# Finer steps in the opening of an attention and feed-forward kernel: a cell's maximum, high part and output product a slot behind its first product

## The chip, the cores and the metric

The kernel runs on one core of one Trainium2 chip. The metric is the device time of one execution, in microseconds, as the median over runs. TensorE is called PE here, VectorE DVE, ScalarE ACT, GpSimd POOL, and SP is the engine whose queue issues nearly all DMAs.

## The reference

Sliding-window attention (8 batches, 8 heads, 576 positions, head size 64, window 64) is followed by a feed-forward layer with a leaky rectifier over all 4608 tokens:

```python
scores = scale * np.matmul(q, k.transpose(0, 1, 3, 2))
mask = (rel >= 0) & (rel < 64)                  # rel = query position - key position
scores = np.where(mask, scores, -1e9)
attn = softmax(scores)                          # with 1e-9 added to the sum
x = (attn @ v) -> (4608, 512)
h = x @ w_in                                    # 512 x 2048
g = np.maximum(h, 0.0) + alpha * np.minimum(h, 0.0)
out = (g @ w_out).astype(np.float32)            # 2048 x 512
```

`w_in` and `w_out` arrive as 64-bit floats, so the kernel reads each weight as two 32-bit halves and rebuilds it. Products are made in a 32-bit format of reduced precision, so every factor is split into a high and a low part and a product is three matmuls: low by high, high by low, high by high.

## The kernel before

The 4608 tokens are 36 tiles of 128. Tiles are grouped into blocks of two (blocks 0, 1 and 2) and three (the ten others). The feed-forward work of a block is 16 cells, one for each 128 of the 2048 hidden columns.

A cell is made of these pieces: `m_hidden` (12 matmuls, tile `h`, line 304), `m_slopes` (ACT multiplies by the scaled slopes, line 313, then DVE takes the maximum, line 314, tile `g`), `m_split` (ACT copies the high part `gh`, line 323, POOL subtracts it for `gl`, line 324) and `m_out` (for each tile of the block three matmuls into `o`, line 338; `gl` is read first).

Weights come in 32 chunks of 512 KB, even ones of `w_in`, odd ones of `w_out`; chunks 2f and 2f+1 belong to cell f. A chunk is fetched into `raw` (three buffers, SP's queue), then turned into 32-bit parts: `mask_exp` (DVE masks the exponent bits into `two`, line 123, ACT rescales them, line 125), `mask_man` (DVE `man`, line 130, ACT, line 133), `join` (DVE `exp`, line 140, and `val`, line 142; two buffers each), `product` (POOL, line 148), `high_part` (ACT, line 159, `win_h` or `wout_h`) and `low_part` (POOL, line 163, `win_l` or `wout_l`).

Attention of a tile: `a_score` (32 matmuls of half the array, in two halves of 16), `a_soft` for each of eight groups (DVE adds the mask and takes the least, line 223; ACT exponentiates and sums, line 226), `a_norm` (DVE adds 1e-9 and inverts, lines 232 and 233; POOL scales `w`, line 234), for the first six tiles `a_transpose_pe` (four PE transposes and an ACT copy for each half), and `a_value` (32 matmuls, ACT copies `xh`, line 262, DVE subtracts for `xl`, line 263).

The opening covers attention of tiles 0 to 5, all 32 chunks, and blocks 0 and 1. In it every engine, and SP's queue, gets its instructions in the order in which the program calls these functions (`tc.manual_schedule()`); an instruction waits for the one ahead of it on its engine even where its own data are there. After a written-out start for tiles 0 and 1, a loop over slots j = 3, 4, ... handles in each slot one chunk's masks, the join and product of the chunk before, high and low part of the one before that, zero to two cells, and one of five attention steps (`STEPS`) of tiles 2 to 5. The first step of a tile also issues the eight loads of the next tile on SP's queue, behind that slot's `fetch`. Block 1's cells begin ten slots after block 0's; until it has caught up there are two cells in a slot. Behind the opening only PE's order is written out, and the blocks 2 to 12 run with the weights resident.

Three PSUM pools matter: `ps_h` (two banks, shared by `h` and `two`), `ps_a` (three banks, shared by `man`, attention's tiles and the output tile `o_3`) and `ps_o` (three banks).

Of the kernel before, what the change touches and what calls it, by code (L numbers as in the profile page):

```python
# [8 lines left out]
F32 = mybir.dt.float32  # L9
# [16 lines left out]
def banded_attention_then_prelu_ffn(  # L26
# [93 lines left out]
    def mask_exp(c):  # L120
        d = cv[c]
        d["two"] = two = ps_h.tile([P, E], I32, tag="ph", name=f"two_{c}")
        nc.vector.tensor_scalar(out=two, in0=d["high"], scalar1=0x7FF00000, scalar2=None,  # L123
                                op0=ALU.bitwise_and)
        nc.scalar.activation(two, two, AF.Relu, scale=8.0, bias=ebias)  # L125

    def mask_man(c):
        d = cv[c]
        d["man"] = man = ps_a.tile([P, E], I32, tag="psa", name=f"man_{c}")
# [3 lines left out]
        nc.scalar.activation(man.bitcast(F32), man, AF.Copy,  # L133
                             scale=s20_sb[:, c // 2:c // 2 + 1] if c % 2 else 2.0**-20)

    def join(c):
        d = cv[c]
        d["val"] = val = io.tile([P, E], F32, tag="val", name=f"val_{c}", bufs=2)
        d["exp"] = exp = io.tile([P, E], I32, tag="exp", name=f"exp_{c}", bufs=2)
        nc.vector.scalar_tensor_tensor(out=exp, in0=d["high"], scalar=-2**31, in1=d["two"],  # L140
                                       op0=ALU.bitwise_and, op1=ALU.bitwise_or)
        nc.vector.scalar_tensor_tensor(out=val, in0=d["low"],
                                       scalar=s52_sb[:, c // 2:c // 2 + 1] if c % 2 else 2.0**-52,
                                       in1=d["man"].bitcast(F32), op0=ALU.mult, op1=ALU.add)
# [72 lines left out]
    def a_soft(t, g):  # L217
# [3 lines left out]
        w, nm = d["w"][:, g, :], d["nm"][:, g:g + 1]  # L221

        nc.vector.tensor_tensor_reduce(  # L223
            out=w, in0=d["s"][u % len(d["s"])][:, e], in1=mask, op0=ALU.add, op1=ALU.min,
            scale=-SCALE, scalar=3.0e38, accum_out=nm)
        nc.scalar.activation(w, w, AF.Exp, scale=-1.0, bias=nm, accum_out=d["sm"][:, g:g + 1])  # L226

    def a_norm(t, halves=(0, 1)):
# [3 lines left out]
        nc.vector.tensor_scalar_add(rc, d["sm"][:, g], 1e-9)  # L232
        nc.vector.reciprocal(rc, rc)  # L233
        nc.gpsimd.tensor_tensor(out=w, in0=w, in1=rc.unsqueeze(2).broadcast_to(list(w.shape)),  # L234
                                op=ALU.mult)

# [7 lines left out]
    def a_transpose_pe(t, u):  # L244
        tp = a_bank(t, f"t_{t}_{u}")
        for e in range(NP):
            nc.tensor.transpose(tp[:, e], st[t]["w"][:, u * NP + e, :], ident)  # L247
        nc.scalar.copy(pts[t % 2][:, u * NP:(u + 1) * NP, :], tp)

    def a_value(t):  # L250
# [4 lines left out]
        for e in range(NP):  # L255
            for u in range(2):
                for h in range(2):
                    r = slice(h * D, (h + 1) * D)
                    nc.tensor.matmul(av[r, e, u * W:(u + 1) * W], v[:, e, u, r],  # L259
                                     pt[:, u * NP + e, h * W:(h + 1) * W], start=True, stop=True)  # L260
        xs = slice((place[n] + i) * P, (place[n] + i + 1) * P)
        nc.scalar.copy(xh[:, :, xs], av)
        nc.vector.tensor_tensor(out=xl[:, :, xs], in0=av, in1=xh[:, :, xs].bitcast(F32), op=ALU.subtract)  # L263
        st.pop(t)

    def eighth(s):
# [17 lines left out]
        elif k == 7:  # L284
# [3 lines left out]
            if last:  # L288
                a_value(t - 1)
            if t + 1 < NT:  # L290
                v_load(t + 1)
# [17 lines left out]
    def m_slopes(n, f):  # L309
# [3 lines left out]
        nc.scalar.activation(g, ph[:, :nt], AF.Copy, scale=sa_sb[:, f:f + 1])  # L313
        nc.vector.scalar_tensor_tensor(out=g, in0=ph[:, :nt], scalar=s_sb[:, f:f + 1], in1=g,  # L314
# [40 lines left out]
    def cell(n, f):  # L355
        m_hidden(n, f)
        m_slopes(n, f)
        m_split(n, f)
# [10 lines left out]
    def load(t):  # L369
# [4 lines left out]
    STEPS = [  # L374
        lambda t: (load(t + 1), a_score(t, (0,)), soft(t, 0)),
        lambda t: (a_score(t, (1,)), soft(t, 1), a_norm(t, (0,))),
        lambda t: (a_norm(t, (1,)), a_transpose_pe(t, 0)),
        lambda t: (a_transpose_pe(t, 1),),
        lambda t: (a_value(t),),
    ]  # L380
    LEAD = 3

    def opening():
# [43 lines left out]
        a_value(1)  # L427

        done, wait = [0, 0], []
        first = [0, 5 * sizes[1]]  # L430
        j = LEAD
        while done != [NF, NF] or wait:

            ready = [n for n in range(2) if j - LEAD >= first[n]]
            at = min(NF, (j - LEAD) // 2 + 1)
            behind = sum(at - done[n] for n in ready)
            cells = []
            for _ in range(min(behind, 2 if behind > 2 else 1)):
# [36 lines left out]
            j += 1  # L475

# [61 lines left out]
```

## Time and profile before

| | |
|---|---|
| median of 3 runs | 976.8 us (976.49 to 978.27) |
| profiled execution | 977.33 us, span 975.5 us, mean granted clock 0.99 |
| busy over the span | PE 922.1 us, DVE 463.1, ACT 423.6, POOL 350.8 |
| opening, up to its last output product | 184.0 us, PE busy 138.1 us in it |
| behind it, to the end of the span | 791.5 us, PE busy 783.9 us in it |

Times in the profile are microseconds from the start of the span. A row of the table of stages gives a stretch, its length, the busy time of each engine with its number of instructions, the granted PE clock as a share of full speed, the mean busy share of the 16 DMA engines and GB/s. A row of the chain of waits gives a start, a duration and the piece of work that the end is traced back to; "issue" is time in which nothing that the profile shows was waited for. A row of a timeline gives start, duration, engine, line, operation, written and read tile, and in brackets the idle time before it and who ended it.

### The profile page before, as it was taken

The page shows a single profiled execution, that of the slowest core. Times are in us where ns is not written, and L with a number is a line of the kernel's source. Part 1 is how long each engine was busy: PE and PEld are TensorE (multiplying, and loading weights), DVE is VectorE, ACT ScalarE, POOL GpSimd, SP SyncE. Part 2 cuts the span into 40 slices and gives each one's busy share as a digit, 9 for nine tenths or more (in the row PEclk, how much of TensorE's full clock was granted, in tenths as well). Part 3 has the DMA queues.
Part 4 walks back from the last instruction along what each step waited for, and adds up shares of the span by engine and source line. Part 5 has one row for each costly group of instructions (what it writes and reads, how often), then busy time and mean ns, then how long its engine had stood idle before and what let it go on. Part 6 is the DMA issues. An engine that isn't in the chain of part 4 may idle for free.

```text
span 975.5 us, 17299 instructions
## 1 busy us (share of the span) xinstructions
PE 922.1 (95%) x6576; PEld 815.7 (84%) x6576; DVE 463.1 (47%) x1394; ACT 423.6 (43%) x1174; POOL 350.8 (36%) x327
## 2 busy tenths in 40 slices
PE   4667988999999999999999999999999999999998
PEld 3456867778898898889889889889988988989997
DVE  3675678576444444444444444444444444441111
ACT  4565676635433433433433443443443344332322
POOL 3575779533233233233233223223223222322221
PEclk9989999999999999999999999999999999999999
DMA  9866284324333233233233233233233232000000
GB/s 212 166 166 150 85 207 141 104 60 93 76 65 62 64 68 64 65 64 65 64 65 65 63 65 65 61 64 69 59 70 64 61 67 53 34 22 1 33 1 33
DMA packets 96418, 74.53 MB, mean 76 GB/s; under 512 B 44624, under 2 KB 89680, under 8 KB 96336
## 3 DMA queue, kind: packets, MB, share of 16 engines
q1 hardware_dynamic: 94272, 73.42, 32.2%
q8 instruction: 52, 0.85, 0.4%
q10 hardware_dynamic: 2064, 0.01, 0.1%
q14 instruction: 30, 0.25, 0.1%
HBM read 63.97 MB, written 9.44 MB: 75 GB/s over the span
## 4 chain that ended last, share of the span: by engine, by line
PE 84%; ACT 6%; DVE 4%; POOL 2%; issue 2%; DMA 1%; SPq 1%; POOLq 0%; ACTq 0%; DVEq 0%
PE h L304 38%; PE o L338 38%; PE s L209 4%; PE av L259 4%; ACT w L226 2%; DVE pt L242 1%; DVE two L123 1%; ACT two L125 1%; ACT g L313 1%; POOL w L234 1%; PE t L247 1%; ACT man L133 1%; ACT gh L323 1%; DMA v<-vN 1%; DVE g L314 1%
## 5 line engine op out<-in xcount | busy, mean ns | idle before, releaser
L324 POOL TENSOR_TENSOR gl<-g,gh 128x384 fp32r<-128x384 f32 (+1 forms) x208 | 196.9, 947 | 428.5 <-ACT gh L323 333.3
L314 DVE SCALAR_TENSOR_TENSOR g<-h,s_sb,g 128x384 f32<-128x384 f32 (+1 forms) x208 | 122.1, 587 | 332.7 <-ACT g L313 329.8
L338 PE MATMUL o<-wout_h,gl 128*128 128x512 f32 x576 | 228.3, 396 | 14.7 <-POOL gl L324 14.7
L338 PE MATMUL o<-wout_l,gh 128*128 128x512 f32 x576 | 229.1, 398 | 0.0
L338 PE MATMUL o<-wout_h,gh 128*128 128x512 f32 x576 | 226.6, 393 | 0.0
L313 ACT ACTIVATE g<-h,sa_sb 128x384 f32<-128x384 f32 (+1 forms) x208 | 115.4, 555 | 251.4 <-PE h L304 251.4
L304 PE MATMUL h<-xh,win_l 128*128 128x384 f32 (+1 forms) x832 | 177.6, 336 | 13.8 <-DVE g L314 6.4
L242 DVE STREAM_TRANSPOSE pt<-w 32x256 f32<-32x256 f32 x360 | 157.0, 436 | 64.2 <-POOL w L234 59.1
L323 ACT CAST gh<-g 128x384 fp32r<-128x384 f32 (+1 forms) x208 | 101.4, 487 | 185.4 <-DVE g L314 185.3
L304 PEld LDWEIGHTS h<-xh,win_l 128*128 128x128 f32 x832 | 141.3, 190 | 36.7 <-DVE g L314 11.9
L304 PE MATMUL h<-xl,win_h 128*128 128x384 f32 (+1 forms) x832 | 169.7, 325 | 0.0
L304 PE MATMUL h<-xh,win_h 128*128 128x384 f32 (+1 forms) x832 | 168.8, 324 | 0.0
L304 PEld LDWEIGHTS h<-xl,win_h 128*128 128x128 f32 x832 | 143.4, 189 | 0.2 <-DVE xl L263 0.2
L304 PEld LDWEIGHTS h<-xh,win_h 128*128 128x128 f32 x832 | 140.6, 190 | 0.0
L338 PEld LDWEIGHTS o<-wout_h,gl 128*128 128x128 f32 x576 | 109.2, 190 | 32.6 <-POOL gl L324 16.0
L226 ACT ACTIVATE w<-w,nm 128x128 f32<-128x128 f32 x288 | 112.3, 392 | 55.7 <-DVE nm L223 55.6
L338 PEld LDWEIGHTS o<-wout_h,gh 128*128 128x128 f32 x576 | 109.5, 190 | 24.4
L234 POOL TENSOR_TENSOR w<-w,rc 128x1024 f32<-128x1024 f32 (+1 forms) x40 | 69.0, 1726 | 160.8 <-DVE rc L233 151.8
L338 PEld LDWEIGHTS o<-wout_l,gh 128*128 128x128 f32 x576 | 109.4, 190 | 14.4
L223 DVE CUSTOM_DVE_ANT_0 w<-s,masks 128x128 f32<-128x128 f32 x288 | 64.1, 286 | 64.4 <-PE s L209 64.3
L209 PEld LDWEIGHTS s<-k,q 64*64 64x64 f32 x1152 | 38.0, 138 | 26.4 <-PE o L338 11.1
L209 PE MATMUL s<-k,q 64*64 64x128 f32 x1152 | 49.5, 285 | 11.1 <-DMA q<-qT 9.0
(43 smaller groups left out, 509.6 us busy)
## 6 DMA issues: line engine op xcount, KB each, us to landing
k<-kT SPq DMA_DIRECT2D x72, 256.0 KB, 4.6
v<-vN SPq DMA_DIRECT2D x72, 256.0 KB, 4.7
q<-qT SPq DMA_DIRECT2D x144, 64.0 KB, 4.3
out<-os SPq DMA_DIRECT2D x36, 256.0 KB, 2.1
raw<-w_in SPq DMA_DIRECT2D x16, 512.0 KB, 4.4
raw<-w_out SPq DMA_DIRECT2D x16, 512.0 KB, 3.6
alpha_sb<-alpha ACTq DMA_DIRECT2D x1, 8.0 KB, 4.6
```

The lines of the kernel that those rows point to most:

```text
L209: nc.tensor.matmul(d["s"][u - halves[0]][out_, e], q[r, e, h, :], k[r, e, :, h, :], start=True, stop=True)
L223: nc.vector.tensor_tensor_reduce(out=w, in0=d["s"][u % len(d["s"])][:, e], in1=mask, op0=ALU.add, op1=ALU.min, scale=-SCALE, scalar=3.0e38 ...
L226: nc.scalar.activation(w, w, AF.Exp, scale=-1.0, bias=nm, accum_out=d["sm"][:, g:g + 1])
L234: nc.gpsimd.tensor_tensor(out=w, in0=w, in1=rc.unsqueeze(2).broadcast_to(list(w.shape)), op=ALU.mult)
L242: nc.vector.transpose(pt[ks, :, r], w[r, :, ks])
L259: nc.tensor.matmul(av[r, e, u * W:(u + 1) * W], v[:, e, u, r], pt[:, u * NP + e, h * W:(h + 1) * W], start=True, stop=True)
L304: nc.tensor.matmul(ph[:, :nt], wt[:, c, fs], xt[:, c, xs], start=(k == 0), stop=(k == 3 * NP - 1))
L313: nc.scalar.activation(g, ph[:, :nt], AF.Copy, scale=sa_sb[:, f:f + 1])
L314: nc.vector.scalar_tensor_tensor(out=g, in0=ph[:, :nt], scalar=s_sb[:, f:f + 1], in1=g, op0=ALU.mult, op1=ALU.max)
L323: nc.scalar.copy(gh, g)
L324: nc.gpsimd.tensor_tensor(out=gl, in0=g, in1=gh.bitcast(F32), op=ALU.subtract)
L338: nc.tensor.matmul(po[t], gt[:, ts], wt[:, f, :], start=(f == 0 and k == 0), stop=(f == NF - 1 and k == 2))
```

## The change

The opening's order is written anew from smaller pieces; what is computed is the same. `a_soft` becomes `a_least` and `a_exp`, `a_norm` becomes `a_inverse` and `a_scale`, `a_transpose_pe` becomes `a_turn` and `a_turned`, `a_value` gives up its two evictions to `a_xh` and `a_xl`, `m_slopes` gives up the maximum to `m_larger`, and the two masks of a chunk are one function, `masks_of`. In the new loop

- a cell's first product is issued at the end of a slot, its slopes at the start of the next, its maximum and split in the middle of that one, and its output product in a later slot (a second cell of a slot is done within it, at the end);
- a chunk's masks and join stand in one slot, its product, high and low part in the next;
- an attention step's PE part comes first in its slot, DVE's least in the middle, ACT's part near the end.

The start for tiles 0 and 1 is reordered too, and the small operations on `alpha` go ahead of the first softmax. A second call of `high_part(1)` and `low_part(1)`, which the loop before made in its first slot, is gone. The core of the diff, new functions first:

```diff
+    def step(t, k):
+        G = range(NP)
+        u = k % 2
+        if k < 2:
+            return dict(pe=lambda: a_score(t, (u,)),
+                        inverse=(lambda: a_inverse(t, (0,))) if k else None,
+                        scale=(lambda: a_scale(t, (0,))) if k else None,
+                        least=lambda: [a_least(t, u * NP + e) for e in G],
+                        act=lambda: [a_exp(t, u * NP + e) for e in G],
+                        dma=(lambda: load(t + 1)) if not k else None)
+        if k < 4:
+            return dict(pe=lambda: a_turn(t, u), act=lambda: a_turned(t, u),
+                        inverse=(lambda: a_inverse(t, (1,))) if k == 2 else None,
+                        scale=(lambda: a_scale(t, (1,))) if k == 2 else None)
+        return dict(pe=lambda: a_value(t), act=lambda: a_xh(t), last=lambda: a_xl(t))
...
         fetch(1)
         v_load(1)
         fetch(2)
+        nc.vector.tensor_scalar(out=s_sb, in0=alpha_sb, scalar1=1.0, scalar2=-2.0, op0=ALU.is_gt, op1=ALU.mult)
+        nc.vector.tensor_scalar_add(s_sb, s_sb, 1.0)
+        nc.vector.tensor_tensor(out=sa_sb, in0=s_sb, in1=alpha_sb, op=ALU.mult)
+        nc.vector.tensor_scalar_mul(s20_sb, s_sb, 2.0**-20)
+        nc.vector.tensor_scalar_mul(s52_sb, s_sb, 2.0**-52)
         a_score(0)
         soft(0, 0)
         soft(0, 1)
-        mask_exp(0)
-        mask_man(0)
-        a_norm(0)
-        nc.vector.tensor_scalar(out=s_sb, in0=alpha_sb, scalar1=1.0, scalar2=-2.0, op0=ALU.is_gt, op1=ALU.mult)
-        nc.vector.tensor_scalar_add(s_sb, s_sb, 1.0)
-        nc.vector.tensor_scalar_mul(s20_sb, s_sb, 2.0**-20)
-        nc.vector.tensor_scalar_mul(s52_sb, s_sb, 2.0**-52)
-        nc.vector.tensor_tensor(out=sa_sb, in0=s_sb, in1=alpha_sb, op=ALU.mult)
+        a_norm(0, (0,))
+        masks_of(0)
+        a_norm(0, (1,))
+        a_turn(0, 0)
+        a_turned(0, 0)
+        a_score(1)
+        soft(1, 0)
         join(0)
+        product(0)
         fetch(3)
-        product(0)
-        a_score(1)
-        a_transpose_pe(0, 0)
-        a_transpose_pe(0, 1)
+        load(2)
+        a_turn(0, 1)
+        a_turned(0, 1)
+        soft(1, 1)
+        a_norm(1, (0,))
+        a_norm(1, (1,))
+        a_value(0)
         high_part(0)
-        soft(1, 0)
-        soft(1, 1)
-        a_value(0)
         low_part(0)
-        mask_exp(1)
-        mask_man(1)
-        a_norm(1)
-        load(2)
+        masks_of(1)
+        a_xh(0)
+        a_xl(0)
+        a_turn(1, 0)
+        a_turned(1, 0)
+        a_turn(1, 1)
+        a_turned(1, 1)
         join(1)
+        product(1)
         fetch(4)
-        product(1)
-        mask_exp(2)
-        mask_man(2)
-        a_transpose_pe(1, 0)
-        a_transpose_pe(1, 1)
+        a_value(1)
+        a_xh(1)
+        a_xl(1)
         high_part(1)
         low_part(1)
-        a_value(1)
-
-        done, wait = [0, 0], []
-        first = [0, 5 * sizes[1]]
+        masks_of(2)
+        join(2)
+        fetch(5)
+
+        done = [0, 0]
+        first = [0, LEAD + 5 * sizes[1]]
+        wait = []
+
+        def pick(j):
+            ready = [n for n in range(2) if j >= first[n] and 2 * done[n] + 2 <= j and done[n] < NF]
+            if not ready:
+                return None
+            n = min(ready, key=lambda n: done[n])
+            done[n] += 1
+            return n, done[n] - 1
+
+        def behind(j):
+            return sum(min(NF, j // 2) - done[n] for n in range(2) if j >= first[n])
+
+        def output(j):
+            if wait and 2 * wait[0][1] + 3 <= j:
+                m_out(*wait.pop(0))
+
+        todo = pick(LEAD - 1)
+        m_hidden(*todo)
         j = LEAD
-        while done != [NF, NF] or wait:
-
-            ready = [n for n in range(2) if j - LEAD >= first[n]]
-            at = min(NF, (j - LEAD) // 2 + 1)
-            behind = sum(at - done[n] for n in ready)
-            cells = []
-            for _ in range(min(behind, 2 if behind > 2 else 1)):
-                n = min(ready, key=lambda n: done[n])
-                cells.append((n, done[n]))
-                done[n] += 1
-            if cells:
-                m_hidden(*cells[0])
-            if 0 <= j - 2 < 2 * NF:
-                high_part(j - 2)
-            if j - 1 < 2 * NF:
-                join(j - 1)
-            fetch(j + 2)
-            if j - 2 < 2 * NF:
-                low_part(j - 2)
-            if cells:
-                m_slopes(*cells[0])
+        while todo or wait or j <= 2 * NF:
+            t, k = divmod(j - LEAD, 5)
+            att = step(t + 2, k) if t + 2 < EARLY else {}
+            part = lambda name: (att.get(name) or (lambda: None))()
+            part("pe")
+            if todo:
+                m_slopes(*todo)
+            if j < 2 * NF:
+                masks_of(j)
             if j - 1 < 2 * NF:
                 product(j - 1)
+            part("inverse")
+            part("scale")
+            output(j)
+            if todo:
+                m_larger(*todo)
+                m_split(*todo)
+                wait.append(todo)
+            part("least")
+            if j - 1 < 2 * NF:
+                high_part(j - 1)
+                low_part(j - 1)
             if j < 2 * NF:
-                mask_exp(j)
-            if cells:
-                m_split(*cells[0])
-            if j < 2 * NF:
-                mask_man(j)
-            if wait and 2 * wait[0][1] + 1 + LEAD <= j:
-                m_out(*wait.pop(0))
-            for c in cells[1:]:
-                m_hidden(*c)
-                m_slopes(*c)
-                m_split(*c)
-                if wait and 2 * wait[0][1] + 1 + LEAD <= j:
-                    m_out(*wait.pop(0))
-            wait += cells
+                join(j)
+
+            if behind(j - 1) > 1:
+                more = pick(j - 1)
+                m_hidden(*more)
+                output(j)
+                m_slopes(*more)
+                m_larger(*more)
+                m_split(*more)
+                wait.append(more)
+            todo = pick(j)
+            if todo:
+                m_hidden(*todo)
             while len(wait) > 2:
                 m_out(*wait.pop(0))
-            t, k = divmod(j - LEAD, 5)
-            if t + 2 < EARLY:
-                STEPS[k](t + 2)
+            part("act")
+            part("last")
+            fetch(j + 3)
+            part("dma")
             j += 1
+        assert done == [NF, NF] and not wait
 
     with tc.manual_schedule():
         opening()
```

More of the change, by code (lines that the diff above doesn't have):

```diff
@@ L118, in fetch, with masks_of @@
         cv[c] = dict(low=raw[:, :, 0].bitcast(U32), high=raw[:, :, 1])
-    def mask_exp(c):
+    def masks_of(c):
         d = cv[c]
         d["two"] = two = ps_h.tile([P, E], I32, tag="ph", name=f"two_{c}")
+        d["man"] = man = ps_a.tile([P, E], I32, tag="psa", name=f"man_{c}")
         nc.vector.tensor_scalar(out=two, in0=d["high"], scalar1=0x7FF00000, scalar2=None,
@@ L125, in mask_exp @@
         nc.scalar.activation(two, two, AF.Relu, scale=8.0, bias=ebias)
-    def mask_man(c):
-        d = cv[c]
-        d["man"] = man = ps_a.tile([P, E], I32, tag="psa", name=f"man_{c}")
         nc.vector.tensor_scalar(out=man, in0=d["high"], scalar1=0xFFFFF, scalar2=0x100000,
@@ L137, in join @@
         d = cv[c]
-        d["val"] = val = io.tile([P, E], F32, tag="val", name=f"val_{c}", bufs=2)
         d["exp"] = exp = io.tile([P, E], I32, tag="exp", name=f"exp_{c}", bufs=2)
@@ L141, in join @@
                                        op0=ALU.bitwise_and, op1=ALU.bitwise_or)
+        d["val"] = val = io.tile([P, E], F32, tag="val", name=f"val_{c}", bufs=2)
         nc.vector.scalar_tensor_tensor(out=val, in0=d["low"],
@@ L215, in a_score, with a_least @@
             d["rc"] = wk.tile([P, NH], F32, tag="rc", name=f"rc_{t}")
-    def a_soft(t, g):
+    def a_least(t, g):
         d = st[t]
@@ L220, in a_soft, with a_exp, a_inverse, a_scale @@
         mask = masks[:, 1 if (t * P + u * W) % seq == 0 else 0, :]
-        w, nm = d["w"][:, g, :], d["nm"][:, g:g + 1]
         nc.vector.tensor_tensor_reduce(
[L224 to L228, printed above, removed]
+            out=d["w"][:, g, :], in0=d["s"][u % len(d["s"])][:, e], in1=mask, op0=ALU.add, op1=ALU.min,
+            scale=-SCALE, scalar=3.0e38, accum_out=d["nm"][:, g:g + 1])
+    def a_exp(t, g):
+        d = st[t]
+        w = d["w"][:, g, :]
+        nc.scalar.activation(w, w, AF.Exp, scale=-1.0, bias=d["nm"][:, g:g + 1],
+                             accum_out=d["sm"][:, g:g + 1])
+    def a_soft(t, g):
+        a_least(t, g)
+        a_exp(t, g)
+    def a_inverse(t, halves=(0, 1)):
+        d = st[t]
+        g = slice(halves[0] * NP, (halves[-1] + 1) * NP)
+        nc.vector.tensor_scalar_add(d["rc"][:, g], d["sm"][:, g], 1e-9)
+        nc.vector.reciprocal(d["rc"][:, g], d["rc"][:, g])
+    def a_scale(t, halves=(0, 1)):
         d = st[t]
@@ L231, in a_norm @@
         w, rc = d["w"][:, g, :], d["rc"][:, g]
-        nc.vector.tensor_scalar_add(rc, d["sm"][:, g], 1e-9)
-        nc.vector.reciprocal(rc, rc)
         nc.gpsimd.tensor_tensor(out=w, in0=w, in1=rc.unsqueeze(2).broadcast_to(list(w.shape)),
                                 op=ALU.mult)
+    def a_norm(t, halves=(0, 1)):
+        a_inverse(t, halves)
+        a_scale(t, halves)
     def a_transpose(t, h, i):
@@ L242, in a_transpose, with a_turn, a_turned @@
             nc.vector.transpose(pt[ks, :, r], w[r, :, ks])
-    def a_transpose_pe(t, u):
-        tp = a_bank(t, f"t_{t}_{u}")
+    def a_turn(t, u):
+        st[t]["tp"] = tp = a_bank(t, f"t_{t}_{u}")
         for e in range(NP):
             nc.tensor.transpose(tp[:, e], st[t]["w"][:, u * NP + e, :], ident)
-        nc.scalar.copy(pts[t % 2][:, u * NP:(u + 1) * NP, :], tp)
+    def a_turned(t, u):
+        nc.scalar.copy(pts[t % 2][:, u * NP:(u + 1) * NP, :], st[t]["tp"])
     def a_value(t):
@@ L260, in a_value, with a_xh, a_xl @@
                                      pt[:, u * NP + e, h * W:(h + 1) * W], start=True, stop=True)
+        st[t]["av"] = av
+    def a_xh(t):
+        n, i = tiles[t]
         xs = slice((place[n] + i) * P, (place[n] + i + 1) * P)
-        nc.scalar.copy(xh[:, :, xs], av)
-        nc.vector.tensor_tensor(out=xl[:, :, xs], in0=av, in1=xh[:, :, xs].bitcast(F32), op=ALU.subtract)
+        nc.scalar.copy(xh[:, :, xs], st[t]["av"])
+    def a_xl(t):
+        n, i = tiles[t]
+        xs = slice((place[n] + i) * P, (place[n] + i + 1) * P)
+        nc.vector.tensor_tensor(out=xl[:, :, xs], in0=st[t]["av"], in1=xh[:, :, xs].bitcast(F32),
+                                op=ALU.subtract)
         st.pop(t)
@@ L289, in eighth @@
                 a_value(t - 1)
+                a_xh(t - 1)
+                a_xl(t - 1)
             if t + 1 < NT:
@@ L313, in m_slopes, with m_larger @@
         nc.scalar.activation(g, ph[:, :nt], AF.Copy, scale=sa_sb[:, f:f + 1])
+        gs[n, f] = ph, g
+    def m_larger(n, f):
+        nt = len(blocks[n]) * P
+        ph, g = gs[n, f]
         nc.vector.scalar_tensor_tensor(out=g, in0=ph[:, :nt], scalar=s_sb[:, f:f + 1], in1=g,
@@ L357, in cell @@
         m_slopes(n, f)
+        m_larger(n, f)
         m_split(n, f)
@@ L371, in load @@
         v_load(t)
[L374 to L380, printed above, removed]
+    def step(t, k):
[13 more added lines that the diff above has]
+        return dict(pe=lambda: a_value(t), act=lambda: a_xh(t), last=lambda: a_xl(t))
     LEAD = 3
```

## The prediction

> **What bounds the kernel now.** I read the table of stages first, cut at the opening's slots (each slot's exponent mask, DVE `two`, opens a row), then the chain of waits, POOL's timeline in the last slots and the waits of the first slots. The columns are the stretch, its length, the busy time of each engine, the granted clock, the busy share of the DMA engines and GB/s.
>
> ```profile
> core 0: us, PE busy (x) PEld busy (x) DVE busy (x) ACT busy (x) POOL busy (x), PEclk, DMA share, GB/s
> 0.00:37.50 37.50, 18.51 (x172) 14.69 (x172) 15.34 (x58) 16.43 (x49) 15.82 (x22) 1.00 0.91 183
> 37.50:85.90 48.40, 31.10 (x223) 24.67 (x218) 33.95 (x89) 30.46 (x78) 32.59 (x29) 0.82 0.66 158
> 85.90:119.30 33.40, 32.12 (x246) 27.45 (x246) 19.76 (x52) 21.27 (x54) 21.19 (x23) 1.00 0.46 118
> 119.30:142.60 23.30, 19.68 (x163) 15.96 (x162) 18.28 (x47) 16.61 (x44) 18.30 (x18) 1.00 0.84 203
> 142.60:171.20 28.60, 24.50 (x144) 19.86 (x144) 24.70 (x42) 19.35 (x40) 25.34 (x24) 1.00 0.48 148
> 171.20:184.00 12.80, 12.21 (x75) 10.06 (x74) 4.14 (x8) 6.97 (x14) 8.48 (x9) 1.00 0.05 17
> ```
>
> Slots 3 to 12 are the second row (48.4 us, ten slots), slots 13 to 17 the third (33.4, two cells a slot), 18 to 22 the fourth (23.3, one cell and attention), 23 to 30 the fifth (28.6, one cell), then 12.8 us of drain. PE is the bound only in the third row: 32.12 of 33.40. Elsewhere in the loop no engine is full: the fullest has 33.95 of 48.40 (DVE), 19.68 of 23.30 (PE), 25.34 of 28.60 (POOL). What sets a slot there is a loop of waits through several engines. One slot of the fifth row, in the chain of waits:
>
> ```profile
> 146.93 0.66 ACT two L125
> 147.59 0.32 ACT gh L323
> 147.91 0.49 ACT man L133
> 148.40 0.16 ACT wout_h L159
> 148.55 0.28 issue
> 148.83 0.48 ACT g L313
> ```
>
> After DVE's mask come ACT's exponent, `gh`, mantissa, high part and slopes in a row, then DVE's maximum, and only then the next mask, one slot on. Nothing of the next slot can start before this one's last step. POOL in the same slot:
>
> ```profile
> 145.47 1.27 POOL L163 TENSOR_TENSOR win_l<-val,win_h 128x512 fp32r<-128x512 f32 x1 [0.35 <-ACT win_h L159]
> 146.71 1.29 POOL L148 TENSOR_TENSOR val<-val,exp 128x512 f32<-128x512 f32 x1
> 147.99 0.74 POOL L324 TENSOR_TENSOR gl<-g,gh 128x256 fp32r<-128x256 f32 x1
> 149.01 1.30 POOL L163 TENSOR_TENSOR wout_l<-val,wout_h 128x512 fp32r<-128x512 f32 x1 [0.28 <-ACT wout_h L159]
> 150.26 1.31 POOL L148 TENSOR_TENSOR val<-val,exp 128x512 f32<-128x512 f32 x1
> ```
>
> Product to product is 3.55 us, though POOL's three pieces need 25.34 / 8 = 3.2: it idles 0.28 before `wout_l`, which waits for ACT's high part. In the first slots the waits are longer:
>
> ```profile
> PE o L338 <- POOL gl L324: 14.7, 5, 4.0
> ACT two L125 <- DVE two L123: 9.2, 9, 2.1
> ```
>
> PE's output product waits 14.7 us in all, for POOL's `gl`, and ACT's `two` 9.2 us for a mask that DVE can't start because it stands behind the maximum of a cell whose first product is not done.
>
> **The change, part by part.** *Prologue.* Before slot 3, tile 1's softmax is followed by tile 0's `xl` and the masks of chunk 1, and its normalization comes behind them:
>
> ```profile
> 20.63 3.08 ACT w L226 x16
> 24.21 0.69 DVE xl L263
> ...
> 26.55 1.91 POOL w L234
> ...
> 33.59 2.94 PE h L304 x12
> 37.47 0.70 DVE two L123
> ```
>
> Tile 1's eight exponentials run from 20.63 to 23.71 on ACT, `xh` and `xl` of tile 0 follow, then the masks, and only then inverse and scaling. In the new order four of the exponentials no longer stand behind the second transposed copy and chunk 0's high part, and both inverses stand ahead of `xl`. I estimate the exponentials' end some 2.8 us earlier, at 20.9; an inverse of 0.4 and a scaling of half a tile, 1.04 (two fences down), give 22.4 for the last scaling's end instead of 26.55 + 1.91 = 28.5. About 1 us of these 6 goes to the masks of chunk 1 and `xh`, now between on ACT: first product near 28.5 instead of 33.59. From there to slot 3's mask it is 3.9 us now. In the new order masks and join of chunk 2 lie beside the first product, but ACT's slopes stay ahead of `two`, so some 3 us remain: 31.5 for 37.47, a gain of 6.0. Ends: 3 (this stretch moves 183 GB/s at a DMA share of 0.91, so transfers can take half of it back) and 7.5. The five small operations on alpha go ahead of the softmax, in DVE's wait for the first scores: nothing. The second `high_part(1)`/`low_part(1)` at slot 3 disappears: it lay beside the path, nothing.
>
> *The slots.* `hidden` goes to the end of the slot before, so that slopes, which come first on ACT, and `m_larger` no longer wait for PE inside the slot; a chunk's join goes to the slot of its masks, high and low part to one slot behind them. PSUM's banks turn over as before (exponent and `h` alternate; mantissa and one attention bank beside `o_3`): nothing. The weight parts thus exist one slot ahead of the product that reads them, and `h` no longer waits for `win_l`. The cross-engine loop that is left runs over two slots: `gl` of a cell, its output product at the next slot, the first product behind it, slopes, `two`, mantissa, `gh`, `gl`. For the rest I need PE's prices, four exponentials, a scaling, and a DVE operation beside POOL:
>
> ```profile
> 78.12 2.93 PE o L338 x6
> ...
> 89.48 1.55 ACT w L226 x8
> ...
> 105.02 1.38 PE o L338 x6
> 106.39 1.47 PE h L304 x12
> ```
>
> ```profile
> 130.03 1.30 POOL L148 TENSOR_TENSOR val<-val,exp 128x512 f32<-128x512 f32 x1
> ...
> 130.71 0.64 DVE L232 TENSOR_SCALAR rc<-sm 128x4 f32<-128x4 f32 x1
> ...
> 132.01 1.04 POOL L234 TENSOR_TENSOR w<-w,rc 128x512 f32<-128x512 f32 x1
> ```
>
> At full clock the loop is 1.38 + 1.47 + 0.48 + 0.66 + 0.49 + 0.32 + 0.74, with 0.3 of gaps 5.8 us for two slots: 2.9 a slot, under POOL's 3.2. So engines, each in its own order, set the slot.
>
> Fifth row: POOL, 3.2 a slot, 25.4 to 25.7 for eight, and 0.3 for the odd miss: 26.0 (ends 25.3 and 28.6). Gain 2.6.
>
> Fourth row, slot by slot of a five-slot tile. k=0: ACT, with four exponentials at the slot's end, 1.55 + 2.4 (19.35 us over eight slots of the fifth row) = 4.0. k=1 and k=2: POOL, 3.2 + 1.0 for the scaling = 4.2 each. k=3: 3.2. k=4: DVE, 24.70 / 8 = 3.1, and 0.6 for `xl`, 3.7. A scaling also waits for its inverse, and the inverse stands on DVE right behind the masks, while POOL has the product: the last fence shows such an `rc` of 4 elements take 0.64 us and end at 131.35, with the POOL operation that began at 130.03 (1.30 long). I add 0.37 to k=1 and k=2 for that. Behind the waiting inverse stand the maximum, and through it `gh`, `gl`. Together 20.0, with some unevenness 20.4 (ends 19.7 and 23.3). Gain 2.9.
>
> The Trainium skill (SBUF — State Buffer, Who interferes with whom) says that a `tensor_scalar` in a two-port mode and a GpSimd operation exclude each other for the whole of whichever began first; the 0.64 us row agrees. By that rule, which speaks against this change, an inverse put right behind the product's start could wait the whole 1.3 us, about 0.6 more for each of eight inverses, and the sum would come out near 960.
>
> Second row: the same sum with half a cell a slot: 3.6, 4.2, 4.2, 2.9, 3.4, so 18.3 for five and 36.6 for ten. PE adds to it. At the lower clock of this stretch (0.82 on average) an output product takes 2.93 and a first product 2.94 (33.59, above) for 1.38 and 1.47; with one tile step of about 1 us on PE the two-slot loop becomes 5.8 + 3.0 + 1 = 9.8 at worst and 6.8 at best, against 7.3 for two slots. Mostly it stays covered; I take 39.0 (ends 34.0, DVE's busy time, and 48.4). Gain 9.4.
>
> By the skill (TensorE: Matmul & The Clock Gate, What's actually happening) TensorE drops to half rate after about 3.4 us of idling and returns after as long a busy time; the row of 0.82 and the doubled 2.93 agree. By it the shorter gaps would leave PE warm, this stretch would be 36.6, and the sum 2.4 lower.
>
> Third row: PE stays the bound, 32.1 busy; 33.0, gain 0.4 (ends 0 and 1.3). Drain: both orders have three more slots behind the last mask; low part and join are a slot earlier, but the two last cells' chains through ACT, DVE and POOL remain: 12.0 for 12.8, gain 0.8.
>
> *Transfers.* Eight loads of a tile stand on SP's queue ahead of the next weight chunk, as now. The slowest case of the kind:
>
> ```profile
> raw<-w_out SPq DMA_DIRECT2D x1, 512.0 KB, 6.4
> ```
>
> Such a chunk is issued about 5.6 us after the slot k=0 ends (eight issues of 0.6 and the fetch's own), lands 6.4 later, and is needed three slots later, 4.2 + 4.2 + 3.2 = 11.6: late by 0.4, inside the unevenness. The fetch of chunk j+3 behind chunk j's join frees the same buffer as that of j+2 behind j-1's now: no other wait. Over all weight chunks the landing time spreads like this:
>
> ```profile
> DMA to landing us min/median/max: 3.1/3.9/8.5
> ```
>
> *Sum.* 6.0 + 9.4 + 0.4 + 2.9 + 2.6 + 0.8 = 22.1 us off the profiled execution. That execution took 977.33 (span 975.5 and 1.8 around it), 0.5 over the median of the runs, 976.8. So 955.2, and as a median 954.7; I say 955. After the opening the rest is an almost full PE and moves along unchanged.
>
> **The rivals.** *Every stage falls to its fullest engine:* 30.0 + 34.0 + 32.1 + 19.7 + 25.3 + 11.5 = 152.6 for 184: 31 off, 946. For it: the new order gives each engine a slot of lead, and the buffers (two of `val`) allow it. Against: in-order engines whose peak changes from slot to slot don't average.
>
> *The first ten slots stay bound by PE at half clock:* the 9.8 us for two slots equals the 9.7 of now, the 9.4 us are not won: 964. For it: in even slots PE does an output product and a first product in a row, and ACT's slopes, at the head of its slot, block both masks behind them. Against: gaps get shorter.
>
> *Weight chunks come late:* 6.4 to 8.5 us to land instead of 4, four tiles, 2.4 us each: 10 back, 964. Against: the 0.4 worked out above, and a median of 3.9.
>
> *Inverses wait out POOL's product:* each of the eight waits the whole 1.3 us, 0.6 more than taken, and scaling, maximum and `gl` move with it: 4.8 back, 960. For it: in the new order the inverse comes right as the product runs. Against: POOL lags behind DVE, so the inverse should as often meet a gap. (It is the skill's rule on the shared port, above.)
>
> *Slower:* the two-slot loop closes in one slot. If an output product stood in the slot of its own cell, `gl` would gate it, it would gate the next first product, this the slopes and the masks: 5.8 us in each of 13 one-cell slots, 75.4 for the 51.9 of rows four and five. Less the 15.4 won before, 8 slower: 985. It decides from two thirds of those slots on. Against: `output(j)` takes a cell that was listed a slot earlier.
>
> *Given back behind the opening:* block 2's attention sets a fixed date there by its loads; 977. Against: they are issued only as the opening ends.
>
> **How the numbers follow.** Forecast 0.53 (its own range 949 to 961); all stages full 0.16; half clock 0.11; waiting inverses 0.08; late chunks 0.05; slower 0.04; no change 0.03. A difference of 0.2%, 2 us, is about what measuring this kernel tells from none. Faster 0.93, same 0.03, slower 0.04. The range runs from the full-engine case to just past the 964 cases: 944 to 967.
>
> **What would show it.** Mask to mask 3.2 to 3.3 us in the last one-cell slots, POOL with hardly a gap; `h` waits for `win_l` no longer; slot 3's mask near 31 to 32; ten slots later near 70; the last mask near 149 to 151, and the rows behind the opening unchanged. Wrong: ACT's slopes waiting for `h` in most slots, long idle times of DVE before masks with a DMA as releaser, `rc` of over 1 us on DVE, or an end of the opening past 170.

## The result and the profile after

The changed kernel takes 956.2 us as a median of four runs (955.0 to 956.6), the kernel before 976.6 in the same comparison: a ratio of 0.9784, 95% interval 0.9769 to 0.9800. The profiled execution took 956.06 us, its span is 954.3 us. The prediction was 955, its range 944 to 967.

The table of stages of the changed kernel, cut again at the exponent masks of slots 3, 13, 18, 23 and 31 and at the last output product of the opening:

```profile
core 0: us, PE busy (x) PEld busy (x) DVE busy (x) ACT busy (x) POOL busy (x), PEclk, DMA share, GB/s
0.00:31.27 31.27, 15.97 (x160) 12.60 (x162) 15.32 (x61) 15.61 (x48) 13.63 (x22) 0.84 1.06 210
31.27:72.13 40.86, 29.64 (x248) 25.49 (x246) 34.42 (x88) 31.03 (x79) 32.47 (x29) 0.83 0.79 194
72.13:101.89 29.76, 28.14 (x220) 24.90 (x214) 20.78 (x52) 19.65 (x51) 21.66 (x23) 1.00 0.61 152
101.89:123.39 21.50, 21.50 (x182) 19.20 (x181) 18.82 (x48) 17.68 (x46) 18.37 (x18) 1.00 0.76 178
123.39:148.38 24.99, 23.77 (x141) 19.93 (x139) 23.53 (x42) 19.37 (x39) 23.93 (x23) 1.00 0.70 184
148.38:163.90 15.52, 14.27 (x103) 11.33 (x102) 4.56 (x9) 8.07 (x16) 10.25 (x11) 1.00 0.10 35
```

| stage | before | after | gain | predicted gain |
|---|---|---|---|---|
| start, to slot 3's mask | 37.5 | 31.3 | 6.2 | 6.0 |
| slots 3 to 12 | 48.4 | 40.9 | 7.5 | 9.4 |
| slots 13 to 17 | 33.4 | 29.8 | 3.6 | 0.4 |
| slots 18 to 22 | 23.3 | 21.5 | 1.8 | 2.9 |
| slots 23 to 30 | 28.6 | 25.0 | 3.6 | 2.6 |
| drain | 12.8 | 15.5 | -2.7 | 0.8 |
| behind the opening, to the end of the span | 791.5 | 790.4 | 1.1 | 0 |
| span | 975.5 | 954.3 | 21.2 | 22.1 |

The chain of waits through the last one-cell slots, where before ACT and DVE took turns, now stays on one engine:

```profile
131.04 1.25 POOL val L146
132.29 0.70 POOL gl L356
...
133.02 1.29 POOL win_l L161
134.32 1.26 POOL val L146
```

POOL's product, `gl` and low part follow each other with gaps of 0.02 to 0.03 us; product to product is 131.04 to 134.32, 3.28 us for 3.55 to 3.59 before. The masks come 3.1 us apart there (24.99 / 8): DVE runs ahead of POOL, and a part of what the masks are ahead is paid behind the last one, in the drain.

In the first ten slots the waits are these:

```profile
PE t L261 <- POOL w L244: 4.4, 2, 2.8
...
PE o L370 <- POOL gl L356: 4.2, 2, 2.6
...
DVE two L124 <- DMA raw<-w_out: 3.4, 1, 3.4
...
DVE two L124 <- DMA raw<-w_in: 1.8, 1, 1.8
```

PE's output products wait 4.2 us for `gl` where it was 14.7. What stands there now, and did not before, are DVE's masks waiting for weight chunks: 3.42 us in slot 7 and 1.84 in slot 12. The chain of waits passes through the first of these chunks, issued at 40.84 behind a tile's loads:

```profile
40.84 7.81 DMA raw<-w_out
```

The end of the opening, on ACT:

```profile
159.19 0.47 ACT L340 ACTIVATE g<-h,sa_sb 128x256 f32<-128x256 f32 x1 [1.67 <-PE h L331]
159.82 1.27 ACT L375 COPY os<-o 128x512 f32<-128x512 f32 x2 [0.15 <-PE o L370]
160.99 0.41 ACT L355 CAST gh<-g 128x256 fp32r<-128x256 f32 x1
```

The copies of two finished output tiles (`os`, 1.27 us) stand ahead of the last cell's `gh`, and POOL and PE wait for that.

### The profile page after: what moved, and what is told of

The parts are those of the page before. It is cut to its first block, busy times and chain, and to the rows that moved or that the text cites. A ratio compares the mean times of both kernels' runs of the same rounds, so it can differ in the third digit from the quotient of the medians.

```text
span 954.3 us, 17329 instructions
## 1 busy us (share of the span) xinstructions
PE 915.1 (96%) x6576; PEld 814.6 (85%) x6576; DVE 464.2 (49%) x1398; ACT 423.7 (44%) x1173; POOL 349.4 (37%) x328
## 3 DMA queue, kind: packets, MB, share of 16 engines
q1 hardware_dynamic: 94272, 73.42, 33.4%
## 4 chain that ended last, share of the span: by engine, by line
PE 86%; POOL 4%; DVE 4%; ACT 3%; DMA 2%; SPq 1%; issue 1%; POOLq 0%; DVEq 0%
PE h L331 40%; PE o L370 39%; PE av L275 4%; PE s L207 4%; DVE pt L256 1%; POOL val L146 1%; ACT w L227 1%; POOL gl L356 1%; DMA raw<-w_out 1%; DMA raw<-w_in 1%; POOL w L244 1%; POOL win_l L161 1%; POOL wout_l L161 1%; DVE two L124 1%; DMA q<-qT 0%
## 5 line engine op out<-in xcount | busy, mean ns | idle before, releaser
L331 PE MATMUL h<-xh,win_l 128*128 128x384 f32 (+1 forms) x832 | 175.0, 332 | 6.7 <-DVE g L346 5.8
```

Source lines behind the costliest of these rows:

```text
L331: nc.tensor.matmul(ph[:, :nt], wt[:, c, fs], xt[:, c, xs], start=(k == 0), stop=(k == 3 * NP - 1))
```

## The experiments

Each is compared with the kernel before, as the changed kernel is (0.9784), and the ratio with its 95% interval stands in brackets. The kernel before took 976.5 us beside most of them, and 977.8 beside four (the maximum one place later, the spread loads, the drain's order, the inverse without the addition); for these the ratio says more than the median. "After" in the edits is the changed kernel.

**The start alone and the slots alone.** In the first, the old order of the start is put ahead of the new slots; in the second, the new start ahead of the old slots.

```diff
 # after, old start (shortened)
-a_norm(0, (0,)); masks_of(0); a_norm(0, (1,)); a_turn(0, 0); ...; a_norm(1, (0,)); a_norm(1, (1,)); a_value(0); ...
+masks_of(0); a_norm(0); ...; soft(1, 0); soft(1, 1); a_value(0); a_xh(0); a_xl(0); low_part(0); masks_of(1); a_norm(1); ...
```

> The new slots behind the old order of the start (tiles 0 and 1, chunks 0 to 2); join of chunk 2 and its fetch are kept at the start's end, so that the loop finds the same state. My theory: the start's 6.2 us (slot 3's mask at 31.3 for 37.5) are a gain of their own: about 962, with the masks of slot 3 near 37 and the later stages as long as in the changed kernel. Rival: the first ten slots are paced by transfers that are issued early anyway, so that a later start is caught up there: 956 to 958, with a shorter stretch from slot 3 to slot 13.

> The complement: the new start with the slots of the kernel before, its doubled high and low part of chunk 1 in slot 3 included. My theory: it keeps the start's 6 us and loses the slots' 14: about 970.5, and the two gains add up (with the other run) to the whole 20.4. Rival: the old slots can't use an early start, because their loop of waits begins with the first product and this comes when the last tile's output is there: 975 or more.

Measured: 959.6 us with the old start (ratio 0.9824, 0.9810 to 0.9839) and 971.7 with the old slots (0.9949, 0.9934 to 0.9964). The masks of slot 3, in DVE's timeline with the old start and then with the old slots:

```profile
35.27 0.69 DVE L124 TENSOR_SCALAR two<-raw 128x512 int32<-128x512 int32 x1
```

```profile
32.19 0.69 DVE L123 TENSOR_SCALAR two<-raw 128x512 int32<-128x512 int32 x1
```

The slots' part is the larger by far: 977 to 960 with the old start, 16 to 17 us. The start is worth 3.4 us by the first run and 4.7 by the second, less than the 6.2 of the stage. With the old start and the new slots slot 3's mask already comes at 35.27 in place of 37.47: those 2.2 us are the new slot's, in which the mask no longer stands behind the first cell's maximum. (With the maximum alone moved in the kernel before, further down, this mask comes at 34.90.) My expectation of 962 had counted them to the start. From there on the stages are as long as in the changed kernel to within 0.6 us (41.4, 29.8, 21.5, 25.0), so an early start is not given back to the transfers.

**The maximum ahead of the masks again.**

```diff
 # after
                 m_slopes(*todo)
+                m_larger(*todo)
 ...
-                m_larger(*todo)
                 m_split(*todo)
```

> One part undone: DVE's maximum of a cell stands ahead of the masks again, right behind the slopes; nothing else changes. My theory: this is the larger part of the slots' gain, since the masks wait again for ACT's slopes and ACT for the masks. The loop is then ACT's five pieces, 0.48 + 0.66 + 0.49 + 0.32 + 0.62, and DVE's maximum and mask between, 0.4 + 0.7: 3.6 to 3.7 a slot in slots 23 to 30 as before (25.0 to 28.6), some 3 us more in slots 3 to 12 and 1 in 18 to 22: 962 to 964. Rival: ACT's slopes are ready when DVE comes to them, since the first product is issued a slot ahead; then the place of the maximum is of no weight: 956 to 957.

Measured: 974.5 us (0.9977, 0.9968 to 0.9987). One DVE instruction of 0.48 us, put ahead of the slot's two masks, takes back 18 of the 20 us. The stages of slots 3 to 12, 13 to 17, 18 to 22 and 23 to 30, columns as before:

```profile
32.16:78.04 45.88, 31.97 (x233) 26.90 (x226) 34.71 (x89) 30.52 (x78) 33.45 (x30) 0.78 0.73 185
78.04:112.87 34.83, 30.05 (x231) 25.91 (x229) 19.56 (x51) 20.51 (x52) 20.95 (x21) 1.00 0.46 115
112.87:138.16 25.29, 22.48 (x171) 19.38 (x170) 17.84 (x49) 17.71 (x46) 17.57 (x18) 1.00 0.71 164
138.16:167.10 28.94, 24.04 (x143) 20.39 (x142) 23.94 (x41) 19.72 (x40) 25.27 (x25) 1.00 0.49 148
```

They are longer by 5.0, 5.1, 3.8 and 4.0 us than in the changed kernel. One slot of the last row in the chain of waits:

```profile
141.78 0.69 DVE two L124
...
142.50 0.66 ACT two L126
143.16 0.51 ACT man L130
143.67 0.31 ACT gh L355
143.98 0.45 ACT wout_h L157
...
144.48 0.48 ACT g L340
...
145.38 0.69 DVE two L124
```

This is the old loop again: mask, ACT's exponent, mantissa, `gh`, high part, slopes, DVE's maximum (0.37 between 145.0 and the mask), mask, in 3.6 us as worked out from the rows. The expectation was right about these eight slots and far too low for the others: I had counted nothing in the two-cell slots, because PE was their bound. There PE's share falls from 28.14 of 29.76 to 30.05 of 34.83. In the chain of waits three of the five masks behind the one at 78.04 (98.36, 105.56 and 112.87) start some 0.4 us behind the end of ACT's slopes, so the maximum gates masks there too; the one at 90.79 follows a transfer.

**The maximum one place later in the kernel before.** The same question from the other side, one part of the change alone:

```diff
 # before
             if j < 2 * NF:
                 mask_exp(j)
             if cells:
+                m_larger(*cells[0])          # taken out of m_slopes
                 m_split(*cells[0])
```

> The kernel before with one thing changed: DVE's maximum of a slot's first cell stands behind the exponent mask of that slot in place of ahead of it. My theory, after the maximum's place alone cost 18 us in the changed kernel: the masks no longer wait for ACT's slopes, and the slots lose most of what they lost there even without the other parts; but the first product still waits for the low part within a slot, and ACT's mantissa still stands behind gh. I expect 8 to 12 us of the 20: 965 to 969. Rival: without the earlier weight parts the place of the maximum is of little weight, since the first product comes late anyway: 973 to 977.

Measured: 966.8 us (0.9897, 0.9872 to 0.9922), about 10.5 us of the 20. With 3.4 to 4.7 for the start, some 5 to 6.5 us remain for all the rest of the new order together. By the stages, slots 3 to 12, 13 to 17, 18 to 22 and 23 to 30 take 45.0, 34.0, 20.6 and 25.4 us: the last two are about as short as in the changed kernel, and what is missing lies in the first two (4.1 and 4.2 us). Which part of the order is worth it I did not take apart; the next two runs show why one of its parts can't be undone by itself.

**High and low part a slot later.**

```diff
 # after
-        while todo or wait or j <= 2 * NF:
+        while todo or wait or j <= 2 * NF + 1:
 ...
-            if j - 1 < 2 * NF:
-                high_part(j - 1)
-                low_part(j - 1)
+            if 2 <= j - 2 < 2 * NF:
+                high_part(j - 2)
+                low_part(j - 2)
```

> The other part undone: high and low part of a chunk one slot later again (two slots behind its masks), all else as changed. My theory: first products wait for the low part again in slots with a cell of block 0, as before (4.0 us of PE's waits in slots 23 to 30), and the last weights come one slot of 3.2 us later: 959 to 961. Rival: the slots' whole gain hangs on the earlier weight parts, and the order on DVE is of no weight: 968 to 970. Second rival: PE has slack for it in one-cell slots and only the last slot counts: 957 to 959.

Measured: 1007.0 us (1.0315, 1.0293 to 1.0337), 51 us more than the changed kernel, far outside all that I expected. A piece of its chain:

```profile
167.38 0.72 POOL gl L356
168.10 1.23 POOL win_l L161
...
169.38 2.94 PE h L331 x12
...
172.40 0.47 ACT g L340
...
174.40 0.74 POOL gl L356
175.14 1.26 POOL wout_l L161
...
176.43 0.03 DVE val L140
...
177.09 0.70 DVE two L124
```

In every second slot the chain goes from `gl` through the low part to the first product (2.94 us; the granted clock is 0.84 in slots 23 to 30) and the slopes, and behind them to ACT's exponent, mantissa and the next `gh`. It is what the prediction had as the slower rival, by another edge: not the output product but the weight's low part gates the first product of the same slot. In the slots between, the edge is DVE's `val`: it has two buffers, and the one that `join` takes is freed by the low part of the same slot; the next mask stands behind it. To tell the two apart, the cells too were put a slot later, so that only the second is left:

```diff
 # high and low part a slot later, and
-                     2 * done[n] + 2 <= j
+                     2 * done[n] + 3 <= j
 ...
-            if wait and 2 * wait[0][1] + 3 <= j:
+            if wait and 2 * wait[0][1] + 4 <= j:
 ...                                          # block 1's first slot and the loop's end move along
```

> The kernel with high and low part a slot later, and here the cells too (first and output products a slot later), so that a first product has its weights a slot ahead again. What remains of the undoing is that DVE's join needs the value buffer that the low part of the same slot frees. My theory: of the 51 us that the late parts cost, the 14 us in eight slots in which PE waits for the low part set the loop (5.6 us a slot), and go; what stays is join behind low part, POOL's chain join, product, high, low within about a slot and a half: 3.6 to 4 a slot: 970 to 985. Rival: the value buffer alone closes the loop: 1000 or more. Second rival: all was the first product's wait: 959 to 961.

Measured: 989.1 us (1.0127, 1.0113 to 1.0140). So the first product's wait is 18 of the 51 us, and 33 remain, of which one more slot at the end is about 3. In its chain:

```profile
161.12 0.74 POOL gl L356
161.86 1.27 POOL wout_l L161
...
163.16 0.03 DVE val L140
...
163.82 0.70 DVE two L124
```

`gl`, low part, `val` of the next chunk but one (it starts as the low part ends), then the next mask: 5.0 us a slot. The buffer is the larger of the two, which I had put at 3.6 to 4. In the changed kernel the join takes a buffer whose low part was issued a slot earlier, and in the kernel before too; the two buffers of `val` are enough for that distance. A run with a third buffer, which would show the rest of it, was not made.

**The doubled parts of chunk 1.**

```diff
 # before
-            if 0 <= j - 2 < 2 * NF:
+            if 2 <= j - 2 < 2 * NF:          # both high_part and low_part
```

> The kernel before without the second high and low part of chunk 1, which its slot 3 makes again (0.62 us on ACT, 1.29 on POOL). My theory, as in the prediction: they lie beside the first product of that slot, no change (within 0.7 us of the kernel before). Rival: slot 3's mask came 2.2 us earlier in the changed kernel than with the old start, and part of that is these two: 1.3 us less.

Measured: 976.8 us (1.0006, 0.9995 to 1.0017): no change, as the prediction had it. In the profiled execution slot 3's mask came 1.0 us earlier (36.46), since the first product took 1.95 us there for 2.94, and slots 3 to 17 were longer by 0.8.

**The loads of a tile spread over four slots.**

```diff
 # after
-            part("dma")                      # load(t + 1): eight DMAs in the first slot of a tile
+            if att:
+                load_part(t + 3, k)          # k and q of one half, of the other, v of one, of the other
```

> The changed kernel with the eight loads of the next attention tile spread over four slots (three, three, one and one, each behind that slot's fetch) in place of all eight behind one fetch. My theory: the chunk behind the eight loads comes late because its issue stands behind theirs on SP's queue and its bytes behind theirs (3.42 us of DVE's waits in slot 7, 1.84 in slot 12); spread, both waits go, and slots 3 to 12 take 35.6 to 37 for 40.9: 951 to 953. Rival: the bytes of that stretch, 194 GB/s, are what limits, so the waits only move to other slots: 955 to 957.

Measured: 955.2 us (0.9777, 0.9755 to 0.9801), not told apart from the changed kernel. In the profiled execution slots 3 to 12 take 38.7 us for 40.9, and DVE's waits for chunks go from 5.2 to 1.7 us, but single chunks still land late. The chain of waits passes through one that had one tile load between it and the chunk before it on SP's queue, where the late one of the changed kernel had eight:

```profile
45.32 9.42 DMA raw<-w_out
```

It takes 9.42 us to land, for 7.8. So the issue order on SP's queue was a part of the lateness only. That the bytes of the stretch are the other part, as the rival has it, is not shown: with the addition left out as well, further down, the same stretch moves 220 GB/s in place of 205, is shorter still, and no chunk issued in it takes more than 7.27 us.

**With the drain's order mended as well.** In the slots behind the last weights, `output(j)` stands behind the split.

```diff
 # loads spread, and
-            output(j)
+            if j <= 2 * NF:
+                output(j)
             if todo:
                 ...
+            if j > 2 * NF:
+                output(j)
```

> The changed kernel with the loads spread as in the other run, and in the slots behind the last weights the output product issued behind the cell's split in place of ahead of it, so that ACT's copy of the last high part no longer stands behind the two copies of finished output tiles (1.27 us, and their wait for PE). My theory: 1 to 1.5 us less than with the spread loads alone: 950 to 952. Rival: what comes next, block 2's attention, waits for the output tiles' copies instead: no difference.

Measured: 955.4 us (0.9777, 0.9755 to 0.9799): no difference to the spread loads alone; the theory's 1 to 1.5 us don't show. The last `gh` does come straight behind the maximum now. Counted from the last mask, the opening's last output product ends 0.8 us earlier than with the spread loads alone (14.7 for 15.5), but block 2's first product starts only 0.3 us earlier (17.6 for 18.0). That goes the rival's way; what holds block 2 there I did not separate.

**The inverse without the addition.**

```diff
 # after
-        nc.vector.tensor_scalar_add(d["rc"][:, g], d["sm"][:, g], 1e-9)
-        nc.vector.reciprocal(d["rc"][:, g], d["rc"][:, g])
+        nc.vector.reciprocal(d["rc"][:, g], d["sm"][:, g])
```

> The changed kernel without the 1e-9 that is added to the softmax sums (left out of the computation), so that each inverse is one DVE instruction, the reciprocal, in place of two. In the changed kernel the addition takes 0.49 to 0.84 us in the slots for 0.17 when POOL is idle. My theory: it waits out POOL's instruction, about 0.5 each; the reciprocal alone will either not wait (0.18) or wait in its place; DVE has the time in two of three such slots, so even with no wait no more than 2 us come back: 954 to 956. Rival: the inverse with its wait holds up the scaling and the maximum in eight slots, 0.5 to 0.8 each: 950 to 952.

Measured: 952.7 us (0.9752, 0.9725 to 0.9778). The first instruction of the inverse in the changed kernel and then here (count, and the least, median and largest duration in ns):

```profile
L237 DVE TENSOR_SCALAR rc<-sm x12: 170/624/871, 12.3 to 113.2; 128x4 f32<-128x4 f32 x12
```

```profile
L237 DVE RECIPROCAL rc<-sm x12: 165/172/179, 12.0 to 111.6; 128x4 f32<-128x4 f32 x12
```

The addition waits in ten of twelve places, and in each of these ten it ends 0.02 to 0.03 us behind a POOL instruction. The reciprocal waits in none, though POOL is at work beside it in ten of the twelve. Leaving the addition out is worth 3.5 us by the medians and 3.1 by the ratios, whose intervals just overlap: more than my 2 and less than the rival's 4 to 6. In the profiled execution 1.9 of it lie in the start, where slot 3's mask comes at 29.35 for 31.27. The Trainium skill (SBUF — State Buffer, Who interferes with whom) names `tensor_scalar` among the DVE operations whose two-port mode and a GpSimd operation exclude each other; the addition's row agrees. The reciprocal, which it does not list there, stays out of it.

**Both together.** Loads spread and no addition:

> Both together on the changed kernel: the loads of a tile spread over four slots, and the inverse as a reciprocal alone (the sums are 1 or more, so the 1e-9 left out is below what a 32-bit float of that size can hold). My theory: in the kernel without the addition the waits for late chunks grew (6.4 us in slots 3 to 12 for 5.2), and spreading the loads takes 2 us of such waits, so the two add up: 950.5 to 952. Rival: transfers of that stretch are the limit for both, and the second gives nothing on top: 952.5 to 954.

Measured: 950.1 us (0.9732, 0.9716 to 0.9748), the shortest time of all, and the only run faster than the changed kernel whose interval lies clear of that kernel's. Slots 3 to 12:

```profile
29.07:66.13 37.06, 27.17 (x220) 23.16 (x220) 32.08 (x85) 29.71 (x77) 32.35 (x29) 0.86 0.90 220
```

37.1 us at 220 GB/s and a DMA share of 0.90. The two gains add up: 6.1 us by the medians, for 1.0 and 3.5 of the single runs, and a little below the 950.5 that I had as the end of the range.

**PE's part of the later attention steps behind the output product**, on top of both:

```diff
-            part("pe")
+            if k < 2:
+                part("pe")
 ...
             output(j)
+            if k >= 2:
+                part("pe")
```

> As the run with spread loads and without the addition, and PE's part of the last three attention steps (two transposes, the value product) behind the slot's output product in place of first in the slot. With the loads spread, PE's transposes waited 7.1 us for POOL's scaling in slots 3 to 12, with output and first products behind them. My theory: PE has slack in those slots, so at most 1 us is won, and in the slots with two cells nothing: 950 to 952. Rival: the waits there set the slots' length: 947 to 949.

Measured: 953.4 us (0.9764, 0.9751 to 0.9777), 3.3 us slower than without it. In slots 3 to 12 the transposes no longer stand waiting, but:

```profile
PE o L369 <- POOL gl L355: 10.8, 5, 3.4
```

the output products wait 10.8 us for `gl` (2.7 in the run above), and now the transposes stand behind them. Both theories fell: PE's wait for POOL's scaling (4.6 us in the run above) had cost nothing that moving it could win.

## Why the prediction was right, point by point

*What bounds the slots.* Shown: the maximum's place alone makes 18 us in the changed kernel and 10.5 in the kernel before, by the loop that was read from the chain of waits. That the masks stood behind ACT's slopes and DVE's maximum was the step that carried the sum. That the sum, 22.1, came within 1 us of the span's 21.2 is in part luck: the stages miss by up to 3.5 us in both directions.

*The start.* 6.0 predicted, 6.2 by the stage, the last piece of it by luck. Up to the first product the pieces came as worked out: the exponentials end near 21.0 (20.9 put), the last scaling at 23.3 (22.4 put; its inverse waited for POOL), the first product starts at 28.0 (28.5 put). From there I had 3 us to slot 3's mask because ACT's slopes stay in the way. The chain of waits has it otherwise: it runs through the masks and the join of chunk 2, and the first product is not in it:

```profile
27.97 0.69 DVE xl L287
28.67 0.61 DVE two L124
29.30 0.67 ACT two L126
...
30.06 0.48 DVE exp L136
...
30.67 0.68 DVE val L140
31.35 0.60 DVE two L124
```

And 2.2 of the 6.2 are the first slot's and not the start's; the start by itself is 3.4 to 4.7. The doubled parts cost nothing, as said.

*Slots 3 to 12.* Mis-sized by 1.9. I had added 2.4 for PE at the lower clock. The clock there stays low (0.83 for 0.82), but PE's output products wait 4.2 us in all, for 14.7. The chunk behind a tile's loads I had late by 0.4; two were late, by 3.42 and 1.84. The step that failed is that sum, 5.6 + 6.4 - 11.6. Counted from the fetch ahead of the loads (35.06 and 56.02) it was about 5.8 + 7.8 - 10.3 for slot 7 and 5.8 + 6.7 - 10.7 for slot 12: the landing took 1.4 and 0.3 us longer than I had, and the three slots until the chunk is needed, with their other waits shorter, were 1.3 and 0.9 shorter. The 2.4 too much and the 4.9 too little make 2.5, not far from the 1.9; no run takes the two apart. The rival of late chunks had the mechanism, and about half its price.

*Slots 13 to 17 and the drain.* 0.4 predicted and 3.6 measured, 0.8 predicted and -2.7 measured. Much of this follows from the mark: masks run further ahead of the cells than before, so rows that are cut at masks gain early and give it back later. Slots 13 to 17 hold nine first products for ten before, slots 18 to 22 six for five. In the drain PE is busy for 2.1 us more, with 41 matmuls of first products for 36 and 29 score matmuls of block 2 for 8. From slot 13's mask to the end of the opening it is 98.1 before and 91.8 after, 6.3, where the four terms made 6.7.

*Slots 18 to 22.* 1.8 for 2.9: PE is busy for all of the 21.50 us, so this stage has PE as its bound, with the cell left from the two-cell slots. I had named ACT, POOL and DVE.

*Slots 23 to 30.* POOL at 3.28 us a slot, predicted 3.2 to 3.3.

*The inverse behind POOL.* I had put 0.37 to two slots of each tile: 0.7 us in slots 18 to 22 and 1.5 in the ten of slots 3 to 12. Taking the wait away won about 3, and slot 3's mask came 1.9 earlier, in a start where I had put nothing. The rule that speaks against the change, as the prediction put it, would have made it near 960; the waits it tells of were there, at about half that price: the addition took 0.49 to 0.84 us in the slots, where the whole POOL instruction is 1.3.

*Behind the opening* nothing was given back: 790.4 us for 791.5.

## What to carry to other kernels

Where engines work through a common list in order, look at what stands *behind* a short instruction that waits: here the place of one maximum of 0.48 us, ahead of DVE's mask or behind it, was worth 18 of 20 us in the changed kernel and half of them in the kernel before. Move such a waiting step behind the work that needs nothing of it before anything is made faster; then check how many buffers lie between the step and the one that frees its target, since a part issued one slot later closed a loop through two buffers, which kept some 30 of the 51 us that it cost even with the cells put later too. A stage cut at one engine's marks gains or loses with that engine's lead, so sum over the stages before judging one.

## What the runs showed of the hardware

An addition of 4 elements for each partition on DVE took 0.17 us with POOL idle and up to 0.87 beside a POOL instruction, until that one ended; a reciprocal of the same size took 0.165 to 0.179 in all twelve places, ten of them beside a POOL instruction. Weight chunks of 512 KB took a median of 3.9 us to land in the opening of the kernel before and 4.5 in that of the changed one, and in slots 3 to 12 single ones took 7.8 to 9.4, where the stretch moved 194 to 205 GB/s; in the run that moved 220 GB/s there the longest was 7.27.
